# Moving VectorE's operand pieces within the steps of a fused FNet and GEGLU kernel

## The chip, the cores and the metric

The kernel runs on one core of one Trainium2 chip. The metric is the device time of one execution in microseconds (us), from the first to the last instruction with what lies around them. Five engines work side by side, each through its own queue in order: TensorE (PE: matmuls, with PEld for the loads of its weights), VectorE (DVE in the profile, V in the code), ScalarE (ACT, A in the code), GpSimd (POOL, G in the code) and SyncE (SP, which issues the DMAs). They wait for each other through semaphores only.

## The reference

The input x has 2048 rows of 448 floats.

```python
h  = x + real part of DFT_seq(DFT_hidden(layernorm(x)))       # FNet mixing
xn = layernorm(h)
h2 = h + (gelu(xn @ w_gate) * (xn @ w_up)) @ w_down           # 448 -> 1792 -> 448
```

Every operand is split into a high and a low half-precision part, and each product is three matmuls (high·high, high·low, low·high). Most products are Strassen forms, so sums of operand blocks are made and split too.

## The kernel before, in words

The first part (to about 346 us) is the layer norm and the two Fourier transforms; an arranged list of tasks orders it and the change doesn't touch it. Then come 42 gate-and-up steps, written out by hand in the loop `for t in range(N_GU)` (L1552). A step makes one unit of 128 hidden features for a part of the 2048 rows:

- steps 0 to 13 (`q == 0`): the first two quarters of the rows together, matmuls 512 columns wide;
- steps 14 to 27: the third quarter, 256 wide; steps 28 to 41: the fourth.

A step's matmuls go into three PSUM banks X, Y, Z. X and Z are the same two banks in all steps from 14 on. The pieces, with what follows each on another engine:

- `x_open`, `x_close`: X; then ACT takes the gelu of X into `g1` (L1305), and a copy of X into Y (L1291);
- `z_open`: starts Z (L1251 with pZ). It overwrites the bank, so it waits until the step before has read its Z;
- `y_mid`: ACT copies Y into `u3` (L1310), then V adds Z to it (`plus`, L1261; out `hid` or `hh`). This must have read Z before
- `z_close` adds to Z; then V's second `plus` (L1261, out `c`, the tile c12) reads the finished Z; it sets the bank free for the next `z_open`;
- `y_open`, `y_close`: Y; `y_close` is followed by V's L1327 (out `hid` or `hh`);
- `c_last` (ACT, L1335) and `c_mul` (POOL, in steps 15 to 28 V, L1339) finish the second half of the hidden unit in the next step. In steps 0 to 13 the hidden units are stored to DRAM (`store`, L1323, SP's queue) and loaded again in another layout (`hid_load`, L1351).

Between these pieces stand the matmuls of the down product (`dn_mm`, L1191, out `acc_d`). Its rows come in 8 pairs of row tiles, each over 7 chunks of the hidden dimension; chunk d = 7·pair + n needs hidden units n and n + 7. `CHUNK_COUNT` gives each step from 14 on its one or two chunks; in a step PE does 8, 10 and 3 matmuls of each chunk in three places: `some(0, 8)`, `some(8, 18)`, `some(18, 21)`. Pairs 6 and 7 (chunks 42 to 55) are multiplied after step 41. Before PE can take a chunk, three pieces make its operand:

- `dn_sums(d, E)`: two sums 256 wide (L1362, L1363) on POOL, or on V where E is V, and one 128 wide on V (L1364), into `dn_s`, of which there are `DN_S = 3` buffers;
- `dn_hi(d)`: two conversions on ACT (L108, 256 and 640 wide) into `dn_w`;
- `dn_lo(d)`: two subtractions on V (L112, 256 and 640 wide) into `dn_w`; then the `dn_s` buffer is free.

In a step from 14 on, `nexts` are the chunks of the next step (their `dn_lo`, before `some(0, 8)`), `sums` those of the step after it (`dn_sums`, after `y_mid`). Other work hangs on named places of a step: `at(side, (t, k), ...)` puts it there and `do(t, k)` runs it. `ahead_of` (L1494) does so for eight chunks of the pairs 6 and 7: 42 to 47 with t = 30, 32, 34, 36, 38, 40, and 49, 50 with t = 31, 39. Their `dn_sums` is all on V, in step t; `dn_hi` at the end of step t + 1; `dn_lo` in step t + 2 (chunk 47's in step 41, at the end).

For chunks 0 to 3 the pieces stand in steps 11 to 13 of the `q == 0` branch: `hi` and `lo` of the chunks of step t + 2 after `z_close`, and behind them `dn_sums` of those of step t + 3.

Of the kernel before, what the change touches and what calls it, by code (L numbers as in the profile page):

```python
# [17 lines left out]
NF = DF // P  # L18
# [15 lines left out]
def kernel(  # L34
# [38 lines left out]
    V, A, G, PE = nc.vector, nc.scalar, nc.gpsimd, nc.tensor  # L73
# [682 lines left out]
    def at(t, n, *what):  # L756
        t.setdefault(n, []).extend(what)
# [60 lines left out]
    for k, (i, i2) in enumerate(tiles_of):  # L818
        n = where["F", i]
        if k > 1:  # L820
            t = None
            if k > 2:
                t = fixed(n - 10, 8, "SP", 0.5, lambda u=i // 2: x_load(u), lag=4.5, kind="xload")
            first_pair = -40.0 if k == 2 else 0.0
            own = "0" if k == 2 else ""
            if (i, i2) in by_scalar:
                t = [add("A", 1.75, T[max(n - 6, 0)], lambda c=c, both=(i, i2): x_moments(c, both), begin=T[max(n - 7, 0)] - 13.0, after=[t], kind="xstat") for c in (i, i2)]
            else:
                t = [add("V", 1.35, T[max(n - 6, 0)] + first_pair, lambda i=i, j=i2: x_stats(i, j), begin=T[max(n - 7, 0)] - 13.0, after=[t], kind="xstat" + own)]
            lite = (i, i2) in by_scalar  # L830
            t = add("A", 0.5 if lite else 0.3, T[max(n - 5, 0)] + first_pair, lambda i=i, j=i2: x_root(i, j), after=t, kind="xroot" + own)
            t = chain("V", RSTD if lite else (0.2, 0.1, 0.1, 0.1), T[max(n - 5, 0)] + first_pair, lambda i=i, j=i2: x_rstd_steps(i, j), [t], kind="xrstd" + own)
            t = add("V", 0.15, T[max(n - 5, 0)] + first_pair, lambda i=i, j=i2: x_bias(i, j), after=[t], kind="xbias" + own)
# [6 lines left out]
        for c in (i, i2):  # L840
            n = where["F", c]
            done = [steps[n]] if n in steps else [add("N", 0.0, 0.0, lambda: None, begin=(-1.8, 0.0, 0.1)[n])]
            if is_s(c // 2):
                t = drained = add("A", 1.05, T[n + 1] + 1.5, lambda i=c: feature_high(i), after=done + ring_w[-2:][:1] * (len(ring_w) > 1), kind="fhigh")
                t = chain("V", (0.56, 0.36, 0.36), T[n + 2], lambda i=c: feature_sums(i, V), [t], kind="fsum")
                t = add("A", 1.45, T[n + 2] + 2.0, lambda i=c: sums_high(i), after=[t], kind="shigh")
                t = add("V", 1.7, T[n + 2] + 3.5, lambda i=c: sums_low(i), after=[t], kind="slow")
                ring_w.append(t)
            else:
                if n > 1:  # L850
                    t = add("A", 0.95, T[n + 1] + 1.0, lambda i=c: feature_high(i), after=done, kind="fhighp")
                else:
                    t = done[0]
# [42 lines left out]
    for p in range(N_PASS):  # L896
# [18 lines left out]
        if q < 2:  # L915
# [5 lines left out]
            for k in range(2):  # L921
                high = add("A", (0.65, 1.0)[k], t0 + 22.0 + k, lambda q=q, j=j, k=k: ffn_hi(q, j, (k,)), after=[t], kind="hhi")
                t = high
# [435 lines left out]
    def dn_sums(d, E=G):  # L1359
        t = dn_hid(d)  # L1360
        s = dn_s[d] = fpool.tile([P, 5, P], F32, tag="dn_s", bufs=DN_S, name=f"dn_s{d}")
        E.tensor_add(s[:, 0:2], t[:, 0:2], t[:, 2:4])  # L1362
        E.tensor_sub(s[:, 2:4], t[:, 1:4:2], t[:, 0:4:2])  # L1363
        V.tensor_add(s[:, 4], t[:, 0], t[:, 3])  # L1364
# [8 lines left out]
    def dn_hi(d, place=None):  # L1373
        if place is None:
            place = fpool.tile([P, 2, 7, P], F16, tag="dn_w", bufs=4, name=f"dn_w{d}")
        dn_w[d] = place
        for src, dst in dn_parts(d):
            hi_part(place[:, 0, dst], src)

    def dn_lo(d):  # L1380
        w = dn_w[d]
        for src, dst in dn_parts(d):
            lo_part(w[:, 1, dst], src, w[:, 0, dst])
        dn_s.pop(d)
# [54 lines left out]
    def chunks(t):  # L1439
        return CHUNKS.get(t, ())  # L1440
# [4 lines left out]
    def do(t, k):  # L1445
        for what in side.pop((t, k), ()):
            what()
# [44 lines left out]
                at(side, (t0 + f, k), what)  # L1492

    def ahead_of(d, t, place):  # L1494
        at(side, (t, 6), lambda: dn_sums(d, V))
        at(side, (t + 1, 7), lambda: dn_hi(d, place()))
        at(side, (t + 2, 6) if t + 2 < N_GU else (t + 1, 7), lambda: dn_lo(d))

    for n in range(6):
        ahead_of(6 * NC + n, 2 * NF + 2 * n + 2, lambda n=n: spare(n, 6 * NC + n) if n < 4 else None)  # L1500
# [31 lines left out]
    def late_prep(beat):  # L1532
        for f, k in late_beats.pop(beat, ()):
            gu[f].beat(k)
            after = [v for v in LATE if v > f]
            if k == 2 and after:
                gu_late(after[0])
            if k == 1:
                gw[f] = gu[f].w
            if k == 4:  # L1540
                at(late_stores, beat + 1, f)
        for f in late_stores.pop(beat, ()):
            gu[f].store()
# [8 lines left out]
    for t in range(N_GU):  # L1552
        q, f = STEPS[t]
        ahead = {0: (), 11: (14,), 12: (), 13: (15,), 14: (16,)}.get(t, (t + 3,) if t < NF else (t + 2,))
        for s in ahead:
            if s < N_GU and s not in LATE:
                gw_load(s)
        if t in (N_GU - 2, N_GU - 1):
            hr_load(t - N_GU + 8)
        nxt = GateUp(t + 1) if t + 1 < N_GU else None  # L1560
        if q == 0:
            do(t, 0)
            cur.x_close()
            nxt.x_open()
            if prev:
                prev.c_last()
                prev.c_mul()
                prev.store(0)
            cur.y_mid()
            late_prep(2 * t)  # L1570
            do(t, 1)
            down_prep(2 * t)
            if prev:
                prev.store(1)
            nxt.z_open()
            nxt.y_open()
            cur.y_close()
            cur.z_close()
            if t >= 10:
                for d in chunks({10: NF, 11: NF + 1, 13: NF + 2}.get(t)):  # L1580
                    hid_load(d)
            for d in chunks(t + 2):
                done.add(d)
                dn_hi(d)
                dn_lo(d)
            if t < NF - 1:
                for d in chunks(t + 3):
                    dn_sums(d)
            do(t, 2)
            down_prep(2 * t + 1)  # L1590
            late_prep(2 * t + 1)
            do(t, 4)
        else:
            mms = [(d, k) for d in chunks(t) for k in range(21)]

            def some(a, b):
                n = len(chunks(t))
                for d, k in mms[a * n : b * n]:
                    dn_mm(d, range(k, k + 1))

            do(t, 0)
            prev.c_last()
            if t == NF:
                prev.c_mul()
                for g in range(2):
                    prev.store(g)
                half0.close()
                later = ctx.enter_context(tc.tile_pool(name="later", bufs=1, side="right", reuse_waits="tile"))
                hh[2] = [later.tile([P, 4, TQ], F32, name=f"hh2_{n}") for n in range(NC)]
                ops3.append(ring.tile([P, 2, N_OPS, 2 * P], F16, tag="ops", bufs=1, name="ops3"))  # L1610
                hops[3] = ops3[0][:, 0]
            elif t > 2 * NF:
                prev.c_mul()
            for d in chunks(t + 3):
                if d < 4 * NC and t + 3 < 2 * NF + 2 and d not in hid_in:
                    hid_load(d)
            cur.x_close()
            if t > NF:
                cur.z_open()
            nexts = [d for d in chunks(t + 1) if d not in done]  # L1620
            if t == 2 * NF - 1:
                nexts += [d for d in chunks(t + 2) if d < 4 * NC]
            done.update(nexts)
            sums = [d for d in chunks(t + 2) if d not in dn_w and d not in dn_s]
            if t == 2 * NF - 2:
                sums += [d for d in chunks(t + 3) if d < 4 * NC]
            for d in nexts[:1]:
                if d not in dn_w:
                    dn_hi(d)
                dn_lo(d)  # L1630
            for d in nexts[1:]:
                dn_hi(d)
                dn_lo(d)
            some(0, 8)
            if t == 2 * NF:
                quarter2.close()
                last = ctx.enter_context(tc.tile_pool(name="last", bufs=1, reuse_waits="tile"))
                hh[3] = [last.tile([P, 4, TQ], F32, name=f"hh3_{n}") for n in range(NC)]
            cur.y_mid()
            if NF < t <= 2 * NF:  # L1640
                prev.c_mul(V)
            for d in sums:
                dn_sums(d)
            do(t, 6)
            some(8, 18)
            if nxt:
                nxt.x_open()
            do(t, 1)
            if not nxt:
                some(18, 21)  # L1650
            do(t, 4)
            cur.y_close()
            cur.z_close()
            if nxt:
                some(18, 21)
            do(t, 5)
            for d in chunks(t + 2)[:1]:
                if d not in dn_w and t < N_GU - 1:
                    dn_hi(d)
            if nxt:  # L1660
                nxt.y_open()
            do(t, 2)
            do(t, 3)
            do(t, 7)
        prev, cur = cur, nxt
# [108 lines left out]
```

## Time and profile before

| | |
|---|---|
| three runs | 708.01, 708.12, 710.34 us; median 708.12 |
| the profiled execution | 708.02 us, span of its instructions 706.2 us |
| PE | busy 692.6 us of the span (98%), granted clock 1.00 |
| DVE | 586.6 us (83%) |
| ACT | 416.1 us (59%) |
| POOL | 169.6 us (24%) |
| DMA | 196 GB/s in the mean |

PE is busy almost without a break, so what can be won lies in the few places where its queue stands still: for each the profile names the line that PE waited for. A matmul's row ends when its result has drained, which is later than the moment when the next one may start.

### The profile page before, as it was taken

To read this page: it belongs to the slowest core of one execution; us is meant where nothing else is said; L and a number is where in the kernel's file an instruction comes from. 1 tells how busy PE (TensorE), PEld (TensorE's weight loads), DVE (VectorE), ACT (ScalarE), POOL (GpSimd) and SP (SyncE) were. 2 spreads that over 40 slices of the span, in tenths; PEclk is the share of its full clock that TensorE was granted. 3 is DMA by queue.
4 is the path that set the end of the run, shared out by engine and by line. 5 is a ranking of instruction groups with operands and counts; after the bars stand their busy time and mean duration, and the time that the engine had idled before them with its cause. 6 is when DMAs were issued, how large, how long until landed. Compare 5 with 4: busy or idle time off the path is not lost.

```text
span 706.2 us, 14542 instructions
## 1 busy us (share of the span) xinstructions
PE 692.6 (98%) x5644; PEld 544.7 (77%) x5644; DVE 586.6 (83%) x1112; ACT 416.1 (59%) x800; POOL 169.6 (24%) x198
## 2 busy tenths in 40 slices
PE   8999999999999999999999999999999999999998
PEld 5455769888888888888744444479999989889898
DVE  6998999999998999999367987786888866585686
ACT  5789764756765666476357666454554534454442
POOL 0000000000000000000033443444646454545342
PEclk9999999999999999999999999999999999999999
DMA  9444345567696869677558687897785844544301
GB/s 338 143 105 112 84 154 179 197 223 214 200 240 191 241 204 262 229 228 272 206 162 266 224 246 264 263 284 248 199 245 207 259 130 135 181 152 162 131 28 53
DMA packets 95381, 138.77 MB, mean 196 GB/s; under 512 B 42192, under 2 KB 71120, under 8 KB 95312
## 3 DMA queue, kind: packets, MB, share of 16 engines
q1 hardware_dynamic: 95312, 137.85, 62.7%
q8 instruction: 44, 0.72, 0.4%
q14 instruction: 25, 0.20, 0.1%
HBM read 100.99 MB, written 27.53 MB: 182 GB/s over the span
## 4 chain that ended last, share of the span: by engine, by line
PE 80%; DVE 11%; DMA 5%; issue 1%; ACT 1%; SPq 1%; ACTq 0%; DVEq 0%
PE acc L605 29%; PE acc_d L1191 14%; PE pY L1251 13%; PE pZ L1251 9%; PE pX L1251 8%; PE ab L484 7%; DMA wr<-in_w_seq_dram 2%; DVE ws L114 1%; DMA hid_dram<-hid 1%; DVE dn_w L112 1%; DVE wss L114 1%; DVE wsum L549 1%; DVE ops L112 1%; DVE dn_s L1364 1%; DMA x<-in_x_dram 1%
## 5 line engine op out<-in xcount | busy, mean ns | idle before, releaser
L1251 PEld LDWEIGHTS <-gw 128*128 128x128 f16 x1638 | 160.0, 98 | 82.5 <-issue 7.7
L605 PE MATMUL acc<-b,ws 128*128 128x224 f16 (+1 forms) x1248 | 187.1, 288 | 0.0
L605 PEld LDWEIGHTS <-ws 128*128 128x128 f16 x1248 | 120.8, 98 | 35.6 <-DVE ws L114 0.2
L605 PE MATMUL acc<-b,wss 128*128 128x224 f16 x1152 | 141.9, 259 | 1.1 <-DVE wss L114 1.1
L1191 PE MATMUL acc_d<-wd,dn_w 128*128 128x224 f16 x1050 | 115.5, 259 | 0.0
L605 PEld LDWEIGHTS <-wss 128*128 128x128 f16 x1152 | 110.8, 98 | 1.4 <-DVE wss L114 1.4
L1191 PEld LDWEIGHTS <-dn_w 128*128 128x128 f16 x1050 | 101.0, 98 | 1.9
L249 POOL TENSOR_TENSOR wd_s<-wd 128x448 f32<-128x448 f32 x7 | 8.8, 1262 | 376.8 <-DMA wd<-in_w_down_dram 349.1
L1251 PE MATMUL pY<-hops,gw 128*128 128x512 f16 (+1 forms) x476 | 88.8, 326 | 0.0
L108 ACT ACTIVATE wss<-wsum 128x1024 f16<-128x1024 f32 x48 | 50.6, 1055 | 49.6 <-PE acc L605 23.5
L108 ACT ACTIVATE ws<-wr 128x768 f16<-128x768 f32 (+1 forms) x64 | 56.4, 889 | 27.5 <-PE acc L605 13.2
L484 PE MATMUL ab<-wh,xT 128*128 128x448 f16 x352 | 69.1, 352 | 1.4 <-ACT wh L108 0.4
L114 DVE SCALAR_TENSOR_TENSOR ws<-wr,ws 128x768 f16<-128x768 f32 (+1 forms) x64 | 64.9, 1018 | 0.0
L114 DVE SCALAR_TENSOR_TENSOR wss<-wsum,wss 128x1024 f16<-128x1024 f32 x48 | 58.6, 1220 | 6.5 <-ACT wss L108 6.2
L1251 PE MATMUL pZ<-hops,gw 128*128 128x512 f16 (+1 forms) x308 | 59.2, 326 | 1.9 <-DVE hh L1261 1.1
L484 PEld LDWEIGHTS <-xT 128*128 128x128 f16 x352 | 33.9, 98 | 33.5 <-issue 1.9
L1251 PE MATMUL pX<-hops,gw 128*128 128x512 f16 (+1 forms) x308 | 56.9, 326 | 0.0
L112 DVE TENSOR_TENSOR dn_w<-dn_s,dn_w 128x640 f16<-128x640 f32 x50 | 49.9, 998 | 1.8 <-ACT dn_w L108 1.5
L1182 POOL TENSOR_TENSOR hr<-hr,v 128x224 f32<-128x224 f32 x56 | 44.3, 815 | 12.3 <-ACT v L1150 11.9
L1291 ACT ACTIVATE pY<-pX 128x256 f32<-128x256 f32 (+1 forms) x42 | 18.5, 440 | 48.5 <-PE pX L1251 48.5
L108 ACT ACTIVATE dn_w<-dn_s 128x640 f16<-128x640 f32 x50 | 36.5, 729 | 7.7 <-DVE dn_s L1364 6.2
L1261 DVE SCALAR_TENSOR_TENSOR hh<-pZ,u 128x256 f32<-128x256 f32 x28 | 11.8, 420 | 34.4 <-ACT u L1310 34.3
(141 smaller groups left out, 996.1 us busy)
## 6 DMA issues: line engine op xcount, KB each, us to landing
wr<-in_w_seq_dram SPq DMA_DIRECT2D x64, 512.0 KB, 4.4
gw<-w_dram SPq DMA_DIRECT2D x36, 896.0 KB, 5.0
gu_raw<-in_w_gu_dram SPq DMA_DIRECT2D x28, 384.0 KB, 4.2
hid_dram<-hid SPq DMA_DIRECT2D x28, 256.0 KB, 5.0
hid_in<-hid_dram SPq DMA_DIRECT2D x28, 256.0 KB, 5.3
w_dram<-gu_p SPq DMA_DIRECT2D x24, 256.0 KB, 2.7
w_dram<-gw SPq DMA_DIRECT2D x6, 896.0 KB, 5.5
hx<-in_x_dram SPq DMA_DIRECT2D x8, 448.0 KB, 5.2
```

The lines of the kernel that those rows point to most:

```text
L108: A.activation(dst, src, AF.Copy, scale=scale)
L112: V.tensor_sub(dst, src, hi)
L114: V.scalar_tensor_tensor(dst, src, scale, hi, op0=ALU.mult, op1=ALU.subtract)
L249: G.tensor_sub(s[:, 2:4], t[:, 0:2], t[:, 2:4])
L484: PE.matmul(feat[i][r][:, :D], xT[i][:, kx, :], w[:, kw, r * D : (r + 1) * D], start=n == 0, stop=n == 10,)
L549: V.tensor_add(s[:, 0:2], r[:, 0:1].to_broadcast([P, 2, 2 * P]), r[:, 1:3])
L605: PE.matmul(banks[k][:, cols], lhs, rhs, start=k not in begun, stop=stop, skip_group_check=True)
L1182: op(x, x, m)
L1191: PE.matmul(acc[k // 2][:, k % 2 * HD : (k % 2 + 1) * HD], a_of(la, a), b_of(lb, b), start=first and m == 0 and k % 2 == 0, stop=last and ...
L1251: PE.matmul(ps, w[:, wl, wa + ws, :], ops[:, m + ms, :], start=first and n == 0, stop=last and n == len(terms) - 1, skip_group_check=True,)
L1261: V.scalar_tensor_tensor(dst, ps, SC, other, op0=ALU.mult, op1=ALU.add)
L1291: A.activation(self.Y, self.X, AF.Copy)
```

## The change

It moves pieces and changes none of them.

1. `ahead_of`: V's `dn_sums` of the eight chunks goes from the place after `y_mid` (`do(t, 6)`) to the place after `z_close` (`do(t, 5)`, itself moved ahead of `some(18, 21)`, which is PE's alone). Their `dn_lo` goes from `do(t, 6)` to a new place `do(t, 8)` before `some(0, 8)`, so ahead of `y_mid`.
2. Step 27: `hi` and `lo` of chunk 27, formerly third in the list `nexts` ahead of `y_mid`, go behind `z_close` and `do(t, 5)` (the list `behind`). Chunks 25 and 26 stay.
3. Steps 11 to 13: `dn_sums` of chunks 0, 1 goes from the end of step 11 to the place after `y_mid` of step 12, that of chunks 2, 3 from the end of step 12 (behind `lo` of chunks 0, 1) to the place after `y_mid` of step 13.

```diff
     def ahead_of(d, t, place):
-        at(side, (t, 6), lambda: dn_sums(d, V))
+        at(side, (t, 5), lambda: dn_sums(d, V))
         at(side, (t + 1, 7), lambda: dn_hi(d, place()))
-        at(side, (t + 2, 6) if t + 2 < N_GU else (t + 1, 7), lambda: dn_lo(d))
+        at(side, (t + 2, 8) if t + 2 < N_GU else (t + 1, 7), lambda: dn_lo(d))
...
             cur.y_mid()
+            for d in chunks(t + 2):
+                dn_sums(d)
             late_prep(2 * t)
...
                 dn_hi(d)
                 dn_lo(d)
-            if t < NF - 1:
-                for d in chunks(t + 3):
-                    dn_sums(d)
             do(t, 2)
...
             nexts = [d for d in chunks(t + 1) if d not in done]
-            if t == 2 * NF - 1:
-                nexts += [d for d in chunks(t + 2) if d < 4 * NC]
-            done.update(nexts)
+            behind = [d for d in chunks(t + 2) if d < 4 * NC] if t == 2 * NF - 1 else []
+            done.update(nexts + behind)
...
             for d in nexts[1:]:
                 dn_hi(d)
                 dn_lo(d)
+            do(t, 8)
             some(0, 8)
...
             for d in sums:
                 dn_sums(d)
-            do(t, 6)
             some(8, 18)
...
             cur.y_close()
             cur.z_close()
+            do(t, 5)
+            for d in behind:
+                dn_hi(d)
+                dn_lo(d)
             if nxt:
                 some(18, 21)
-            do(t, 5)
```

## The prediction

> **What bounds the kernel now.** I read the page's head first, then the waits of each engine, then the order of time around every wait that TensorE has.
>
> ```profile
> span 706.2 us, 14542 instructions
> PE 692.6 (98%) x5644; PEld 544.7 (77%) x5644; DVE 586.6 (83%) x1112; ACT 416.1 (59%) x800; POOL 169.6 (24%) x198
> ```
>
> PE is the bound. The change touches neither the number nor the shape of an instruction, so it is worth just what it does to PE's standstills. The view of waits, PE's rows:
>
> ```profile
> PE pZ L1251 <- DVE c L1261: 4.4, 4, 1.7
> PE pZ L1251 <- DVE hh L1261: 1.1, 1, 1.1
> PE pZ L1251 <- DVE hid L1261: 0.7, 1, 0.7
> ```
>
> These six are all of PE's waits for VectorE in the 42 steps: four for c12 (the second `plus`, which frees Z for the next `z_open`), two for the first `plus` (which must read Z ahead of `z_close`). The timeline of PE at the places, idle time in brackets:
>
> ```profile
> 575.38 0.71 PE L1251 MATMUL pZ<-hops,gw 128*128 128x256 f16 x5 [1.10 <-DVE hh L1261]
> 614.19 0.81 PE L1251 MATMUL pZ<-ops,gw 128*128 128x256 f16 x6 [0.95 <-DVE c L1261]
> 628.17 0.81 PE L1251 MATMUL pZ<-ops,gw 128*128 128x256 f16 x6 [1.29 <-DVE c L1261]
> 643.42 0.82 PE L1251 MATMUL pZ<-ops,gw 128*128 128x256 f16 x6 [0.54 <-DVE c L1261]
> 657.79 0.82 PE L1251 MATMUL pZ<-ops,gw 128*128 128x256 f16 x6 [1.67 <-DVE c L1261]
> ```
>
> 575.38 is step 27's `z_close`; the other four are the `z_open` of steps 33, 35, 37 and 39, behind the even steps in which `ahead_of` has both a `dn_lo` and a `dn_sums`. Five matmuls make a row of 0.71, six one of 0.82: one adds 0.11, but the last of a row shows about 0.27. So a bracket is 0.16 short of what PE loses, and the five cost 5.55 + 5 × 0.16 = 6.35 us.
>
> **Part 1, the eight chunks of `ahead_of`.** VectorE, ScalarE, POOL and PE in step 32, in that order:
>
> ```profile
> 609.55 0.42 DVE L1261 SCALAR_TENSOR_TENSOR hh<-pZ,u 128x256 f32<-128x256 f32 x1 [2.48 <-ACT u L1310]
> 610.32 0.88 DVE L112 TENSOR_TENSOR ops<-hh,ops 128x256 f16<-128x256 f32 x1
> 611.12 1.28 DVE L112 TENSOR_TENSOR ops<-dn_s,ops 128x640 f16<-128x640 f32 x1
> 612.50 0.43 DVE L1362 TENSOR_TENSOR dn_s<-hh 128x256 f32<-128x256 f32 x1
> 613.39 0.42 DVE L1327 SCALAR_TENSOR_TENSOR hh<-pY,g 128x256 f32<-128x256 f32 x1
> 613.72 0.41 DVE L1261 SCALAR_TENSOR_TENSOR c<-pZ,u 128x256 f32<-128x256 f32 x1
> 614.05 0.42 DVE L112 TENSOR_TENSOR dn_w<-hh,dn_w 128x256 f16<-128x256 f32 x1
> 614.38 0.82 DVE L112 TENSOR_TENSOR dn_w<-dn_s,dn_w 128x640 f16<-128x640 f32 x1
> ...
> 607.04 0.73 ACT L108 ACTIVATE ops<-dn_s 128x640 f16<-128x640 f32 x1
> ...
> 608.15 0.73 POOL L1339 TENSOR_TENSOR hh<-hh,c 128x256 f32<-128x256 f32 x1 [3.87 <-ACT c L1335]
> ...
> 611.04 0.71 PE L1251 MATMUL pZ<-ops,gw 128*128 128x256 f16 x5
> ...
> 618.42 0.71 PE L1251 MATMUL pZ<-ops,gw 128*128 128x256 f16 x5
> ```
>
> PE finishes Z at 611.75, yet c12 starts at 613.72: ahead of it stand chunk 42's `dn_lo` (610.32 to 612.40) and chunk 43's `dn_sums` (612.50 to 613.39). Just before, at the first `plus`, VectorE had stood idle for 2.48 us. The change puts the `dn_lo` into that hole and the `dn_sums` behind c12. The `dn_lo` needs ACT's high part, which is there at 607.77; it takes 1.15 alone (614.05 to 615.20, chunk 33's) or 2.08 beside POOL (610.32 to 612.40), both less than 2.48. Then c12 ends near 612.2, 0.9 before PE wants Z (614.19 − 1.11 = 613.08): the wait goes, here and by the same order in steps 34, 36 and 38. Sum 0.95 + 1.29 + 0.54 + 1.67 + 4 × 0.16 = 5.09 us.
>
> What is late next: the sums now delay what follows c12 on VectorE, the next step's `dn_lo` pieces and then its first `plus`, behind which PE's `z_close` waits. The tightest is step 33, where another `dn_lo` (chunk 49) stands there too. From c12's end at 612.2 to step 33's `z_close` (618.42, moved to 617.3) are 5.1 us; the `plus` takes 0.42 and a little on either side, so 4.6 are left for sums (0.89), chunk 33's `dn_lo` (1.15) and chunk 49's (1.15, or 2.08 beside POOL). That is 3.2 to 4.1: it fits, with 0.5 us in hand at the worst of these rows. The same load comes only in steps 32 and 40 and, with the `dn_lo` of chunks 35 and 36, in step 35. The other directions are covered: the moved chunks are multiplied after step 41, so neither their `dn_hi` a step later nor PE waits; a `dn_s` buffer is now held from c12 of one step to the start of the second next, less long than before. No DMA is issued in these pieces.
>
> How POOL slows VectorE is the weak point. In the rows a subtraction of 0.42 takes 0.88 and one of 0.82 takes 1.28 beside POOL, 0.46 more each. The Trainium skill (SBUF — State Buffer, section "Who interferes with whom") says that a DVE instruction with two SBUF inputs contends with a GpSimd instruction that reads SBUF, and that the second to issue "fully blocks" until the first ends. By that rule a piece could lose a whole POOL instruction of 0.73 each time, and chunk 49's `dn_lo` would take 1.15 + 2 × 0.73 = 2.6, an estimate by that page; step 33 would then need 4.65 of its 4.6, still no loss to speak of. The trace's 0.46 is a part of it, as if the wait began halfway.
>
> **Part 2, chunk 27 in step 27.** VectorE, and ScalarE's `u3`:
>
> ```profile
> 571.51 1.35 DVE L112 TENSOR_TENSOR dn_w<-dn_s,dn_w 128x640 f16<-128x640 f32 x1
> 572.78 0.94 DVE L112 TENSOR_TENSOR dn_w<-hid_in,dn_w 128x256 f16<-128x256 f32 x1
> 573.64 1.34 DVE L112 TENSOR_TENSOR dn_w<-dn_s,dn_w 128x640 f16<-128x640 f32 x1
> 574.91 0.41 DVE L1261 SCALAR_TENSOR_TENSOR hh<-pZ,u 128x256 f32<-128x256 f32 x1
> ...
> 581.22 0.42 DVE L1261 SCALAR_TENSOR_TENSOR hh<-pZ,u 128x256 f32<-128x256 f32 x1 [4.67 <-ACT u L1310]
> ...
> 572.63 0.36 ACT L1310 ACTIVATE u<-pY 128x256 f32<-128x256 f32 x1
> ```
>
> `u3` is ready at 572.99, but the first `plus` stands behind chunk 27's two subtractions until 574.91. Without them it runs at 573.0 and ends at 573.4, before `z_close`'s unhindered start (575.38 − 1.26 = 574.12). The whole 1.10 + 0.16 = 1.26 us goes. Chunk 27's conversions and subtractions land behind c12, two steps before PE takes the chunk; next behind them is the `plus` of step 28, for which VectorE had idled 4.67 us. On ACT the two conversions leave the place ahead of `u3`, which only helps.
>
> **Part 3, chunks 0 to 3.** Here I book nothing, though a wait of 0.72 + 0.16 = 0.88 us goes. In the order of time, the lines are from the timelines of DVE, PE, POOL and ACT, then the chain and the table of stretches:
>
> ```profile
> 462.57 2.09 DVE L1364 TENSOR_TENSOR dn_s<-hid_in 128x128 f32<-128x128 f32 x2
> 482.08 0.29 DVE L1364 TENSOR_TENSOR dn_s<-hid_in 128x128 f32<-128x128 f32 x1 [3.04 <-DMA hid_in<-hid_dram]
> ...
> 465.31 1.24 PE L1251 MATMUL pZ<-hops,gw 128*128 128x512 f16 x5 [0.72 <-DVE hid L1261]
> ...
> 461.92 1.31 POOL L1363 TENSOR_TENSOR dn_s<-hid_in 128x256 f32<-128x256 f32 x1
> 463.19 1.32 POOL L1339 TENSOR_TENSOR hid<-hid,c 128x512 f32<-128x512 f32 x1
> 468.09 1.46 POOL L1339 TENSOR_TENSOR hid<-hid,c 128x512 f32<-128x512 f32 x1 [3.58 <-ACT c L1335]
> ...
> 470.77 7.80 DMA hid_dram<-hid
> 478.65 3.40 DMA hid_in<-hid_dram
> ...
> 483.09 0.82 PE pZ L1251 x6
> ...
> 460.00:465.00 5.00, 4.59 (x31) 2.84 (x29) 5.00 (x7) 3.55 (x8) 3.40 (x3) 1.00 1.01 344
> ```
>
> In step 13 the sums of 2.09 us delay the first `plus`; moved behind it they free `z_close` (465.31). But 18 us later PE stands at 483.09 (step 16's `z_open`) at the end of another chain: unit 13's store at 470.77, 7.80 us of DMA, the load of chunk 6 (3.40), its sum on VectorE at 482.08, c12, `z_open`. That chain hangs on SP's queue and on the DMA engines, busy share 1.01 from 460 to 465 us, not on PE. PE arrives there 0.88 us earlier and waits 0.88 longer. The pieces before it are on VectorE and POOL in steps 12 and 13, so the same chain hides what they may cost, as long as unit 13's product on POOL (to 469.55 now) is done by 470.77. It may slip: the sums of chunks 2 and 3 (now all behind POOL's product of unit 12, which moves up from 463.19 towards 461.9) and so ACT's conversions stand ahead of its gelu. By POOL's rows two chunks take at most 4 × 1.31 = 5.2 us from 463.2, to 468.4, and with a conversion and the gelu (about 0.7 each) the product would end at 471.3: at most 0.5 us late. Bounds: a loss of 0.5, or, if the DMAs move up with unit 12's store, a gain of 0.88; I take zero, since the DMA share shows a full queue.
>
> **The sum.** 5.09 + 1.26 + 0 = 6.35 us. The profiled execution took 708.02, of it 706.2 span: 708.02 − 6.35 = 701.67. It lies 0.1 under the median of the three runs; I forecast 701.7.
>
> **The rivals.**
>
> *The join gains too.* If unit 12's product, 1.3 us earlier on POOL, pulls the store, the load and the next store with it, part 3 keeps its 0.88: 700.8. Against it stands the full DMA queue.
>
> *VectorE is only partly freed.* The moved pieces make the first `plus` late in the tight steps 32, 33, 35 and 40, by as much as the 0.5 in hand is overrun. Were all three pieces beside POOL (sums 0.89 + 3 × 0.46 = 2.27, `dn_lo` 2.08 twice), 6.4 us would stand against 4.6: 1.8 lost in each, and if two of the four do so, 3.6: 705.3. For it: POOL runs three instructions per such step; against it: they start only after ACT's gelu, when most of VectorE's pieces are past.
>
> *The other side, slower.* VectorE loses a whole 0.73 us to POOL in each of the seven pieces (three sums, four subtractions) between c12 and the next first `plus`: 3.2 + 5.1 = 8.3 us against 4.6, 3.7 lost in each of the four steps, 14.8 in all: 708.0 − 6.35 + 14.8 = 716.5. It turns into a loss where the overrun passes 6.35 / 4 = 1.6 us a step, four whole waits and more. This is the blocking rule of the skill page above taken to its end. Against it, no row between 606 and 616 us lost over 0.46, and POOL hasn't seven instructions there.
>
> **How the numbers follow.** The forecast as it stands, 701.0 to 702.8 by the half us at the join and some tenths in tight steps: 0.72. The join gains too: 0.12. Partly freed: 0.12. Slower: 0.04. Leaving out the slow case and the upper half of the partly freed one, the range is 700.5 to 703.6. A measurement of this kernel can tell 0.5%, 3.5 us, from no change: faster than 704.6 are the first two cases and half of the third, 0.90; within 0.5% 0.06; slower 0.04.
>
> **What would show it.** In the trace after: PE's waits for `c` and for `hh` gone from 566 us on; VectorE's `dn_lo` ahead of the first `plus` in the even steps, its 256-wide sums behind c12. In step 13 `z_close` without a wait, and a wait near 483 us of about 0.9, ended by VectorE, with chunk 6's load landing near 482. The prediction is wrong if new PE waits for `hh` stand in steps 32, 33, 35 or 40, or if the load of chunk 6 lands more than half a us off.

## The result and the profile after

| | before | after |
|---|---|---|
| median of 5 runs, us (lowest to highest) | 708.46 (708.01 to 711.46) | 703.44 (701.63 to 705.16) |
| ratio of the times, 95% interval | | 0.9907 [0.9882, 0.9932] |
| profiled execution, us | 708.02 | 701.63 |
| its span, us | 706.2 | 699.9 |

The time fell by 0.93%. The median lies inside the range of 700.5 to 703.6, near its upper end, and above the 701.0 to 702.8 of the forecast as it stands. The profiled execution fell by 6.39 us against the 6.35 of the sum. The median lies 1.8 us above that execution: both kernels' five runs scatter by about 3.5 us, more than the three that the prediction started from.

The head of the page after, TensorE's waits of the 42 steps in the view of waits (total, times, longest), and the timeline of PE at step 15's and step 16's `z_open`, at step 27's `z_close` and at the `z_open` and `z_close` of step 33:

```profile
span 699.9 us, 14545 instructions
PE 691.3 (99%) x5644; PEld 544.8 (78%) x5644; DVE 581.6 (83%) x1112; ACT 416.0 (59%) x800; POOL 169.6 (24%) x198
...
PE pZ L1251 <- DVE c L1261: 1.2, 1, 1.2
...
474.79 0.81 PE L1251 MATMUL pZ<-hops,gw 128*128 128x256 f16 x6 [1.22 <-DVE c L1261]
...
483.06 0.82 PE L1251 MATMUL pZ<-hops,gw 128*128 128x256 f16 x6
...
574.10 0.71 PE L1251 MATMUL pZ<-hops,gw 128*128 128x256 f16 x5
...
611.79 0.82 PE L1251 MATMUL pZ<-ops,gw 128*128 128x256 f16 x6
616.03 0.71 PE L1251 MATMUL pZ<-ops,gw 128*128 128x256 f16 x5
```

Of the six waits of before none is left, and one that was not there has come: 474.79, which is step 15's `z_open`, with chunk 5's sum late. Lining up PE's 5644 matmuls before and after, one by one, gives what each place won: 0.88 at step 13's `z_close`, −1.38 at step 15's `z_open` (bracket 1.22 and 0.16), 0.25 at step 16's `z_open`, 1.26 at step 27's `z_close`, and 1.11, 1.45, 0.70 and 1.83 at the `z_open` of steps 33, 35, 37 and 39. With 0.27 that PE was already ahead before 455 us, where nothing is changed, that is 6.37 us. (Below, "shift" always means this: the start of the same matmul in two traces.)

Why the new wait is where it is, VectorE's timeline of after around it and, below it, that of before with PE's row:

```profile
469.69 0.29 DVE L1364 TENSOR_TENSOR dn_s<-hid_in 128x128 f32<-128x128 f32 x1
473.18 0.29 DVE L1364 TENSOR_TENSOR dn_s<-hid_in 128x128 f32<-128x128 f32 x1 [3.20 <-DMA hid_in<-hid_dram]
...
474.33 0.41 DVE L1261 SCALAR_TENSOR_TENSOR c<-pZ,u 128x256 f32<-128x256 f32 x1
```

```profile
472.47 0.29 DVE L1364 TENSOR_TENSOR dn_s<-hid_in 128x128 f32<-128x128 f32 x1 [0.64 <-DMA hid_in<-hid_dram]
...
473.62 0.41 DVE L1261 SCALAR_TENSOR_TENSOR c<-pZ,u 128x256 f32<-128x256 f32 x1
...
474.56 0.82 PE L1251 MATMUL pZ<-hops,gw 128*128 128x256 f16 x6
```

Before, c12 started at 473.62 and could have released PE 0.46 later (that is the distance 474.33 to 474.79 after), at 474.08; PE came at 474.56: 0.48 us in hand. After, PE comes 1.15 earlier (the 0.88 and the early 0.27) and c12 0.71 later, with its sum: 1.15 + 0.71 − 0.48 = 1.38. The 0.71 comes from a load, as SP's timelines show, before and then after (hid_dram is unit 12's stores, hid_in the loads of chunks 4 and 5; the second of each pair is issued at the end of its row):

```profile
460.94 4.12 SPq L1323 DMA_DIRECT2D hid_dram<-hid  x2
465.15 4.01 SPq L1351 DMA_DIRECT2D hid_in<-hid_dram  x2
```

```profile
460.78 2.74 SPq L1323 DMA_DIRECT2D hid_dram<-hid  x2
463.61 5.80 SPq L1351 DMA_DIRECT2D hid_in<-hid_dram  x2
```

```profile
461.70 1.28 POOL hid L1339
...
463.00 6.04 DMA hid_dram<-hid
...
469.09 4.00 DMA hid_in<-hid_dram
```

The last fence is the chain of waits after: unit 12's product on POOL, its store, chunk 5's load, and behind it the sum at 473.18. The store is issued 1.5 us earlier than before (the first row of SP ends at 463.5, not at 465.1), and still chunk 5's load is issued no sooner (the second row ends at 469.4, not at 469.2). The store landed at 469.03, before the change at 468.79: the DMA engines took the 1.5 us whole.

### The profile page after: what moved, and what is told of

Its sections match the earlier page's. It is cut to its first block, busy times and chain, and to the rows that moved or that the text cites. A ratio compares the mean times of both kernels' runs of the same rounds, so it can differ in the third digit from the quotient of the medians.

```text
span 699.9 us, 14545 instructions
## 1 busy us (share of the span) xinstructions
PE 691.3 (99%) x5644; PEld 544.8 (78%) x5644; DVE 581.6 (83%) x1112; ACT 416.0 (59%) x800; POOL 169.6 (24%) x198
## 4 chain that ended last, share of the span: by engine, by line
PE 84%; DVE 6%; DMA 6%; issue 1%; SPq 1%; ACT 1%; POOL 1%; ACTq 0%; DVEq 0%
PE acc L605 30%; PE acc_d L1191 16%; PE pY L1251 14%; PE pZ L1251 9%; PE pX L1251 9%; PE ab L484 7%; DMA wr<-in_w_seq_dram 2%; DVE ws L114 1%; DMA hid_dram<-hid 1%; DVE wss L114 1%; DMA hops<-xs 1%; DVE wsum L549 1%; DMA x<-in_x_dram 1%; DMA xT<-xs 1%; DMA hid_in<-hid_dram 1%
## 5 line engine op out<-in xcount | busy, mean ns | idle before, releaser
L1182 POOL TENSOR_TENSOR hr<-hr,v 128x224 f32<-128x224 f32 x56 | 42.7, 787 | 12.3 <-ACT v L1150 11.9
L1310 ACT ACTIVATE u<-pY 128x256 f32<-128x256 f32 (+1 forms) x42 | 19.1, 454 | 34.8 <-PE pY L1251 34.7
```

The costliest lines, as they stand in the source:

```text
L1182: op(x, x, m)
L1310: A.activation(u3, self.Y, AF.Copy, scale=SC)
```

## The experiments

Four parts of one theory were to be told apart: that each removed wait is paid out at its own place (parts 1 and 2 of the prediction), that part 3's is given back at a chain of DMAs, that VectorE has room for the moved pieces in the tight steps, and what ends that chain.

**The three parts, each alone.** `e1_ahead` has only `ahead_of`'s edits, `e2_step27` only the list `behind`, `e3_join` only the `dn_sums` of chunks 0 to 3; the rest is as before.

```diff
# e1_ahead, against the kernel before
-        at(side, (t, 6), lambda: dn_sums(d, V))
+        at(side, (t, 5), lambda: dn_sums(d, V))
-        at(side, (t + 2, 6) if t + 2 < N_GU else (t + 1, 7), lambda: dn_lo(d))
+        at(side, (t + 2, 8) if t + 2 < N_GU else (t + 1, 7), lambda: dn_lo(d))
# e2_step27
+            for d in behind:       # behind z_close, formerly in nexts
+                dn_hi(d)
+                dn_lo(d)
# e3_join
             cur.y_mid()
+            for d in chunks(t + 2):
+                dn_sums(d)
```

> The kernel before with part 1 alone (the eight chunks' sums behind c12, their dn_lo ahead of the first plus). Theory that PE's waits simply add up: the four waits at the z_open of steps 33, 35, 37 and 39 go and nothing else does; PE's start after step 39 lies 5.09 us earlier than before (1.11 + 1.45 + 0.70 + 1.83), the span near 701.1, a time near 703.0 where the kernel before has 708.1. Rival that parts 1 and 2 overlap (step 27's wait, left in, leaves more slack later): less than 4.5 us.

> The kernel before with part 2 alone (chunk 27's hi and lo behind step 27's z_close). Adding up: step 27's wait of 1.10 goes, 1.26 us with the matmul's drain, the four later waits stay as they were (0.95, 1.29, 0.54, 1.67); span near 704.9, time near 706.8. Rival: the time won at step 27 comes back in a longer wait of steps 33 to 39, then about 708.

> The kernel before with part 3 alone (the sums of chunks 0 to 3 moved). If the DMA chain sets the time: step 13's z_close no longer waits (PE 0.88 us earlier at 465 us), and by 484 us PE is where it was, within 0.3: no change, about 708.1. If the part costs by itself on VectorE and POOL: step 16's z_open more than 0.5 us later than before, 708.7 or more. If the join gains: 707.3.

| | median, us (runs) | ratio to before | places won, by shift, us |
|---|---|---|---|
| `e1_ahead` | 705.23 (11) | 0.9929 [0.9907, 0.9951] | 1.12, 1.45, 0.70, 1.83 |
| `e2_step27` | 707.84 (12) | 0.9974 [0.9954, 0.9994] | 1.26 |
| `e3_join` | 709.22 (12) | 1.0001 [0.9978, 1.0024] | 0.88, then −1.23 and 0.25 |

The savings add up within the intervals: 0.71% and 0.26% and nothing, against 0.93% for the whole. Parts 1 and 2 are worth what the brackets said, each at its own places; part 3 by itself is no change that can be measured, for the 0.88 is given back nine microseconds later. (The trace of `e2_step27` has two further waits, of 0.52 and 0.36 by shift, at the `z_open` of steps 15 and 16, where it changes nothing, and in that of `e1_ahead` step 27's wait, which it doesn't touch, is 0.51 longer.) The wait that takes it, in the timeline of PE of `e3_join`, and then the same place in `e1_ahead`, where part 3 is not done, with VectorE's sum of chunk 5 ahead of it:

```profile
474.19 0.82 PE L1251 MATMUL pZ<-hops,gw 128*128 128x256 f16 x6 [1.07 <-DVE c L1261]
```

```profile
476.30 0.29 DVE L1364 TENSOR_TENSOR dn_s<-hid_in 128x128 f32<-128x128 f32 x1 [3.02 <-DMA hid_in<-hid_dram]
...
477.91 1.44 PE L1251 MATMUL pZ<-hops,gw 128*128 128x256 f16 x6 [3.49 <-DVE c L1261]
```

So in the profiled execution of `e1_ahead` the same place stood for 3.49 us with the old sums: chunk 5's load was late there by itself (its sum stands at 476.30, where it stood at 472.47 before). The place belongs to the load, and part 3 is one way among others to reach it. That execution of `e1_ahead` took 708.18, 3 us over the median of its own kernel.

**Two ways to take the chain away.** If the wait at step 15 is the DMA queue's, it should go when the queue is lighter. `e4_hr_late` issues the first residual pair's load (448 KB, line 1407, between the stores in step 13) in step 16. If it is only that c12 stands behind the sums, it should go when the sums stand behind c12: `e5_sums_behind` does that with the `dn_sums` of steps 14 and 15. `e6_both` does both.

```diff
# e4_hr_late, against the kernel after
-        at(side, (t0 - 4, 0), lambda p=p: hr_load(p))
+        at(side, (t0 - 4, 0) if p else (t0 - 1, 4), lambda p=p: hr_load(p))
# e5_sums_behind
             for d in sums:
-                dn_sums(d)
+                if t > NF + 1:
+                    dn_sums(d)
...
             cur.z_close()
+            for d in sums:
+                if t <= NF + 1:
+                    dn_sums(d)
             do(t, 5)
```

> The changed kernel with the load of the first residual pair (hr, 448 KB) issued at step 16 instead of step 13. If the full DMA queue ahead of unit 12's store sets the wait at step 15's z_open: its packets (1.4 to 1.5 us of the queue) no longer stand ahead of the store, the load of chunk 5 lands about 1.4 us earlier, the wait of 1.22 (1.38 with the drain) goes to 0 to 0.3, and the span falls from 699.9 to about 698.5, a time near 700.2. If the store's own latency or SP's queue sets it, or the 896 KB weight load ahead of it does: no change (699.9).

> The changed kernel with the sums of chunks 4, 5 and 6 (steps 14 and 15) moved behind c12 as well, so that VectorE no longer stands at a load ahead of c12. If the wait at step 15's z_open comes only from the place of chunk 5's sum in VectorE's queue: that wait (1.38) and step 16's go although the load lands as before; PE 1.4 to 1.6 us earlier after step 16 than the changed kernel, unless ScalarE, which converts chunk 6 ahead of u2, takes 0.3 to 0.6 back: span 698.3 to 699.0. Rival (the late load holds PE by its matmuls): the wait turns up at acc_d of step 16 and the span stays near 699.9.

> The changed kernel with both: hr's first load at step 16 and the sums of chunks 4 to 6 behind c12. Both take away the same wait, so no more than either alone: PE after step 16 1.4 to 1.7 us earlier than in the changed kernel, no wait of PE from 455 us on, median 701.0 to 702.3 where the kernel before has 709.8 in these rounds. If late loads are what spreads the times, the spread of the runs gets smaller than that of the changed kernel (3.5 us over five).

Medians 702.51 (6 runs), 701.97 (4) and 701.81 (5), ratios to before 0.9890 [0.9864, 0.9916], 0.9904 [0.9884, 0.9923] and 0.9895 [0.9876, 0.9913]. In none of the three traces does PE wait at all from 455 us to the end. Step 15's `z_open` and, for the first, chunk 4's and 5's sums on VectorE, now in one row without a wait between them; for the second, VectorE with c12 ahead of the sums:

```profile
471.75 1.21 DVE L1364 TENSOR_TENSOR dn_s<-hid_in 128x128 f32<-128x128 f32 x2
475.50 0.82 PE L1251 MATMUL pZ<-hops,gw 128*128 128x256 f16 x6
```

```profile
473.09 0.42 DVE L1261 SCALAR_TENSOR_TENSOR c<-pZ,u 128x256 f32<-128x256 f32 x1 [0.19 <-PE pZ L1251]
473.44 0.53 DVE L1364 TENSOR_TENSOR dn_s<-hid_in 128x128 f32<-128x128 f32 x2
474.60 0.82 PE L1251 MATMUL pZ<-hops,gw 128*128 128x256 f16 x6
```

In all three the wait is gone. That c12 stands behind the sum is shown by `e5_sums_behind`: the load lands there at 473.58, no sooner than in the kernel after (473.08), and c12 no longer waits for it. The queue's half is less sure. In `e4_hr_late` PE came to this place 2.09 us later than in the kernel after, from waits far ahead of the edit, and that alone eases the wait (in `e9_lo_twice`, 1.65 later with nothing changed here, 0.59 of the 1.22 is left); the store landed at 469.13, no sooner than the 469.03 of after, and only the load behind it was shorter (2.8 us from issue to landing, not 4.0). In `e6_both` PE was on time, the store took 4.0 us in place of 6.0, and the load landed at 469.77, which speaks for the queue. But in a second execution of that kernel (`e12_both_again`, below) the store took 6.2 us again and the load landed at 472.13, only 0.95 us sooner than in the kernel after. So the residual load may be part of what holds chunk 5's load up; how much of it, these traces don't settle. The ratios can't tell the three from the kernel after (0.9907); what the wait's end is worth is read from the traces: `e6_both` has a span of 698.3, 1.6 below. In the profiled executions of `e4_hr_late` and `e5_sums_behind` (spans 700.6 and 699.7) some more waiting ahead of 280 us, where nothing is changed, takes it again: about 1 us of it (1.5 in the first) near 276.

**More load on the queue.** `e10_hr_two` is the dose in the other direction: the second residual pair's load too is issued in step 13.

```diff
-        at(side, (t0 - 4, 0), lambda p=p: hr_load(p))
+        at(side, (t0 - 4, 0) if p != 1 else (NF - 1, 0), lambda p=p: hr_load(p))
```

> The changed kernel with the second residual pair's load (448 KB) also issued in step 13. If the queue ahead of unit 12's store sets the wait at step 15's z_open, 1.4 to 1.5 us of packets more stand in it: the wait of 1.38 grows to 2.8 to 2.9, the span to about 701.3, unless other waits differ. If not the queue: 1.2 to 1.6 as before.

707.01 us (one run), span 705.2. Views of `e10_hr_two`: SP, PE, and stretches of 1 us, where PEclk is the last column but two:

```profile
461.52 2.04 SPq L1407 DMA_DIRECT2D hr<-h_dram  x2
...
465.15 8.66 SPq L1351 DMA_DIRECT2D hid_in<-hid_dram  x2
...
478.75 1.44 PE L1251 MATMUL pZ<-hops,gw 128*128 128x256 f16 x6 [3.64 <-DVE c L1261]
...
478.00:479.00 1.00, 0.24 (x2) 0.18 (x2) 0.70 (x3) 0.93 (x2) 0.71 (x2) 0.64 0.93 373
479.00:480.00 1.00, 1.00 (x7) 0.69 (x6) 0.48 (x2) 1.00 (x3) 0.00 (x0) 0.50 1.04 319
480.00:481.00 1.00, 1.00 (x7) 0.83 (x6) 0.83 (x2) 1.00 (x4) 0.00 (x0) 0.50 0.69 205
```

The place and the direction are as the queue's theory has them: the row of the loads is 8.66 long in place of 5.80, and the wait is 3.64 in place of 1.22. The size is not: 2.4 us more, where 1.4 to 1.5 were expected. And `e1_ahead` waited 3.49 here without the second load, so this one trace doesn't show that the load did it: the scatter of chunk 5's load alone reaches as far. And the standstill was followed by a half clock, of which below.

**The two moves of `ahead_of`.** Which of them frees c12? `e7_lo_only` moves just the `dn_lo`, `e8_sums_only` just the sums (the two halves of `e1_ahead`'s diff).

> The kernel before with only the dn_lo of the eight chunks ahead of the first plus, their sums left where they were. By VectorE's rows the sums alone (0.9 to 2.0 us from the first plus on) are over before PE has finished Z: all four waits go, 5.0 to 5.1 us, as with both moves. Rival (each piece is half of the delay): 2 to 3 us left of the waits.

> The kernel before with only the sums of the eight chunks behind c12, their dn_lo left after the first plus. By the rows the dn_lo (2.1 us beside POOL) ends at 612.4 in step 32 and 626.4 in step 34 (two sums ahead of it): c12 then ends about 0.1 late for step 33 and 0.5 late for step 35, the others in time: 4.4 to 4.5 us of the 5.09. Rival: 2 to 3 us.

705.31 and 703.38 us (one run each). By the shifts at steps 33, 35, 37 and 39, `e7_lo_only` wins 0.94, 0.93, 0.70 and 1.20, together 3.77: the expectation missed. `e8_sums_only` wins 1.07, 1.06, 0.70 and 1.79 and loses 0.17 at step 35's `z_close`: 4.45, as expected. The two overlap (3.77 + 4.45 is far over 5.09), so either does most of the work, and only both do all. What the first lacks, VectorE and PE in step 34 of `e7_lo_only`:

```profile
623.34 0.42 DVE L1261 SCALAR_TENSOR_TENSOR hh<-pZ,u 128x256 f32<-128x256 f32 x1 [0.93 <-ACT u L1310]
623.68 1.57 DVE L1364 TENSOR_TENSOR dn_s<-hh 128x128 f32<-128x128 f32 x2
625.17 0.94 DVE L1362 TENSOR_TENSOR dn_s<-hh 128x256 f32<-128x256 f32 x1
...
626.37 0.28 DVE L1364 TENSOR_TENSOR dn_s<-hh 128x128 f32<-128x128 f32 x1
...
627.37 0.81 PE L1251 MATMUL pZ<-ops,gw 128*128 128x256 f16 x6 [0.35 <-DVE c L1261]
```

With the `dn_lo` gone the sums start right behind the first `plus` and run beside POOL: two small ones of other chunks take 1.57 (one alone takes 0.28, the last row but one), and the three of V 1.48, from 625.17 to 626.65, not the 0.89 of step 32, where they stood behind the `dn_lo`.

**How much room the tight steps have.** `e9_lo_twice` does every moved `dn_lo` twice, the second time writing the same values over the first: nothing is left out, and VectorE's load at the disputed place rises.

```diff
-        ... else (t + 1, 7), lambda: dn_lo(d))
+        ... else (t + 1, 7), lambda: (dn_lo_again(d), dn_lo(d)))
```

> The changed kernel with the moved dn_lo of the eight chunks done twice (the same values written again): 1.15 to 2.1 us more on VectorE ahead of the first plus in steps 32, 33, 34, 36, 38, 40 and 41. By the changed kernel's rows the plus may come 1.06 us later in step 32 and 1.6 to 2.7 us later in the others (its idle time before, and 1.06 from its end to z_close). So PE waits for hh in step 32 by 0.1 to 1.1, in step 33 by at most 0.5, nowhere else: span 0.1 to 1.6 us longer. Rival (POOL blocks VectorE for whole instructions, so that the pieces already fill their room): waits in most of the seven steps, over 3 us.

First the place in the kernel after, VectorE in step 33:

```profile
610.92 0.42 DVE L1362 TENSOR_TENSOR dn_s<-hh 128x256 f32<-128x256 f32 x1
...
613.19 0.81 DVE L112 TENSOR_TENSOR dn_w<-dn_s,dn_w 128x640 f16<-128x640 f32 x1
614.55 0.42 DVE L1261 SCALAR_TENSOR_TENSOR hh<-pZ,u 128x256 f32<-128x256 f32 x1 [0.54 <-ACT u L1310]
```

Then `e9_lo_twice`: POOL's product in step 32, VectorE's pieces in step 33, PE's `z_close`, the clock behind it:

```profile
607.90 2.52 POOL L1339 TENSOR_TENSOR hh<-hh,c 128x256 f32<-128x256 f32 x1 [3.53 <-ACT c L1335]
...
611.94 0.79 DVE L1362 TENSOR_TENSOR dn_s<-hh 128x256 f32<-128x256 f32 x1
612.65 0.88 DVE L1363 TENSOR_TENSOR dn_s<-hh 128x256 f32<-128x256 f32 x1
...
616.86 0.95 DVE L112 TENSOR_TENSOR dn_w<-hh,dn_w 128x256 f16<-128x256 f32 x1
617.73 1.27 DVE L112 TENSOR_TENSOR dn_w<-dn_s,dn_w 128x640 f16<-128x640 f32 x1
618.92 0.41 DVE L1261 SCALAR_TENSOR_TENSOR hh<-pZ,u 128x256 f32<-128x256 f32 x1
...
619.39 0.70 PE L1251 MATMUL pZ<-ops,gw 128*128 128x256 f16 x5 [2.17 <-DVE hh L1261]
...
620.40:621.40 1.00, 1.00 (x7) 0.72 (x6) 1.00 (x3) 0.09 (x1) 0.00 (x0) 0.50 0.99 371
```

707.42 us (one run), span 705.6. Of the steps with a double `dn_lo` only step 33 makes PE wait, by 2.33 where at most 0.5 was expected; step 32, expected to, doesn't, and the rival, waits in most of the steps, isn't seen. In the kernel after, the pieces behind c12 last 3.1 us (610.92 to 614.00) and then VectorE waits 0.54 for ACT; the `plus` ends 1.06 before PE's 616.03, so there are 1.6 in hand. With the double `dn_lo` the same stretch lasts 7.0 (611.94 to 618.92), 3.9 more: 2.3 over, and 2.33 is what PE waited. By VectorE's rows the added pair of subtractions is 2.13 of the 3.9; the sums took 0.85 longer than in the kernel after (0.79 and 0.88 in place of 0.42 each) and the pair of the last rows 0.92 longer. I read the lengthening as contention with POOL, which lies beside these pieces: its product of step 32 (0.73 both in the prediction's row and in the kernel after) took 2.52 while VectorE had subtractions back to back, and so POOL's next pieces came to lie beside VectorE's sums.

**Once more, side by side.** `e11_after_again` is the kernel after and `e12_both_again` is `e6_both`, unchanged, on one chip.

> The changed kernel again, on the chip of the next: 0.9907 of the kernel before, as it was, a median 5 to 7 us under it; the wait at step 15's z_open between 0.5 and 3.5 from run to run.

> The kernel with both join repairs again, beside the changed one: 1.4 to 1.7 us less than it in the profile; in the medians 1 to 3 us less, since late loads no longer hold PE.

703.05 (6 runs; 0.9906 [0.9876, 0.9935]) and 701.29 (6; 0.9881 [0.9853, 0.9909]). The second is the best of all the kernels here by 1.8 us on that chip, but the intervals overlap. In the profile it is 0.9 us shorter (699.5 against 700.4), less than the 1.4 to 1.7 expected. Nor does it scatter less: by 4.3 us, and `e6_both` by 2.9, where the kernel after scatters by 3.5 and 3.7. That late loads spread the times, as the expectation of `e6_both` had it, isn't borne out. The traces show what is left in each, first of `e11_after_again`, then of `e12_both_again`:

```profile
474.32 0.82 PE L1251 MATMUL pZ<-hops,gw 128*128 128x256 f16 x6 [0.69 <-DVE c L1261]
483.57 0.82 PE L1251 MATMUL pZ<-hops,gw 128*128 128x256 f16 x6 [0.81 <-DVE c L1261]
```

```profile
482.12 0.42 ACT L108 ACTIVATE dn_w<-hid_in 128x256 f16<-128x256 f32 x1 [2.72 <-DMA hid_in<-hid_dram]
483.83 0.74 ACT L108 ACTIVATE dn_w<-dn_s 128x640 f16<-128x640 f32 x1 [1.29 <-POOL dn_s L1363]
...
484.88 0.82 PE L1251 MATMUL pY<-hops,gw 128*128 128x256 f16 x6 [0.84 <-ACT u L1296]
```

The kernel after again waits for loads, this time at two places, at 483.57 also for chunk 6, the one that the prediction had named. With both edits a late chunk 6 no longer holds up c12, but ACT, which converts it ahead of step 16's `u`: a load that is late enough holds up the next instruction that stands behind it (1.00 us by shift).

## Why the prediction was right, and where it was not

*Part 1, 5.09 us.* Won 1.11, 1.45, 0.70 and 1.83, with the reason given. The assumption that a bracket falls 0.16 short of what PE loses holds at each of these places. Three of its sizes were off. The 0.5 us in hand at step 33 was 1.6, since neither of the two `dn_lo` there ran beside POOL. The tightest step was 35, which the prediction names beside it: its `plus` ends at 627.94, 0.63 before PE's `z_close`. "Sums 0.89" was read where they stood behind other pieces; beside POOL they took 1.48 (`e7_lo_only`). And the 0.46 that POOL was taken to cost was typical (the last subtraction before step 32's `plus` took 1.36, not 0.82) but not the most. The same form, on VectorE and then POOL in step 14 of the kernel after:

```profile
467.51 1.89 DVE L112 TENSOR_TENSOR dn_w<-dn_s,dn_w 128x640 f16<-128x640 f32 x1
...
467.18 1.55 POOL L1339 TENSOR_TENSOR hid<-hid,c 128x512 f32<-128x512 f32 x1 [1.37 <-ACT c L1335]
```

It lost 1.07 beside a POOL product of 1.55 that started 0.33 ahead of it, and ended 0.67 after it. The ends tell more than the starts. In the prediction's fence the subtraction of 0.82 ends at 612.40, 0.69 after POOL's piece beside it (line 1182, 610.20 to 611.71); in step 32 of the kernel after one ends at 608.28, 0.68 after POOL's product (606.87 to 607.60). So each of them ended as if it had stood until POOL's piece was over and then taken most of its own time: the 0.46 was what was left of POOL's piece, not a wait that began halfway. This agrees with the whole block that the Trainium skill (SBUF — State Buffer, "Summary: rules for kernel authors") states for a DVE instruction with two SBUF inputs beside a GpSimd one that reads SBUF, and not with the "part of it" that the prediction read. By the rule of the same page of the Trainium skill ("Who interferes with whom") that the order of issue decides who blocks, POOL loses in its turn, as `e9_lo_twice` had it. None of this cost PE anything in the kernel after.

*Part 2, 1.26 us.* Won 1.26, in the kernel after and alone.

*Part 3, nothing.* The mechanism held: PE arrived earlier and waited for a load that did not move up. The place didn't: "18 us later PE stands at 483.09" looked only at the next wait that was already there. Nine microseconds later stood a place with 0.48 in hand, less than the 0.88 that PE was to win, and of the same kind (a store, a load, a sum, c12). So the whole 0.88 and 0.50 more was lost at 474.79, the old wait of 0.25 at 483 went, and the term is −0.25, inside its bounds of −0.5 to 0.88. The sign that was named, a wait of about 0.9 near 483 us, didn't come, though chunk 6's load landed where it did before (481.86, and 482.06 before). "Unit 13's product may slip, at most 0.5 late" did not happen (POOL's row above ends at 468.73, and at 469.55 before); the half microsecond came from the DMA engines instead. The rival "the join gains too" fails with the 1.5 us of the earlier store that came to nothing.

*The sum.* That the profiled execution meets it within 0.04 us is luck: part 3's −0.25, booked as nothing, was made good by the 0.27 that PE was early before the change begins. What the moved pieces won themselves is 6.10.

*The other rivals.* Neither "VectorE is only partly freed" nor the slower one is seen: PE has no wait for `hh` in steps 32, 33, 35 and 40. `e9_lo_twice` shows that the mechanism exists and what it takes: 3.9 us more on VectorE, not the lengthening that POOL gives by itself.

*The median.* 1.7 above the forecast. The sum was made against one execution at the low end of its runs, 708.02, and gave 701.67 for one at the low end of the runs after, 701.63. What the other runs have more is not traced. The traces of `e1_ahead` and `e11_after_again` show late loads of chunks 5 and 6, and others an extra 1 us near 276, as sources of such a scatter; how much of it they make stays open.

## What to carry to other kernels

In these traces a wait behind an in-order queue was won in full when the piece ahead of it fitted into a hole of the same engine that is seen in the trace. Count the wait by the start of what follows, and time the moved piece beside whatever POOL runs there. Before booking it, follow the gain forward: not only to the next wait, but to every place whose operand comes from a DMA and which has less in hand than the gain. If such a place is there, move the consumer of the load behind what the bound engine needs, as `e5_sums_behind` does; a lighter DMA queue may help too, but here it did so unevenly.

## What the hardware showed that I had not expected

A long standstill of PE costs more than itself. Behind 3.49 us in `e1_ahead` and 3.64 us in `e10_hr_two` PE's granted clock was 0.50 for about 3.4 us, most of which the stretches above show (0.64, 0.50 and 0.50), matmuls in rows of six took 1.44 in place of 0.82, and the shift grew by another 1.6 and 1.4 us. The Trainium skill (TensorE: Matmul & The Clock Gate, "Part 1: The HAM clock gate") gives half rate after an idle window of about 3.4 us, and the length of the half clock agrees with that figure. But in `e9_lo_twice` 2.33 us of standstill were enough, with the half clock starting 1 us after PE was back, and the shift there grew from 3.36 to 5.02 us while it lasted. The 1.67 us before and the 1.38 after had no such sequel.

The length of one standstill doesn't decide it, though. `e9_lo_twice` has another half clock, from 9.41 to 12.83 us. The clock had risen at 6.00, and no bracket between is over 0.97; `e12_both_again` has 0.96 at the same matmul and keeps its clock. PE's longest standstill there and a stretch of the half clock:

```profile
7.74 0.23 PE L445 MATMUL xT_ps<-ident,xs 128*128 128x128 f16 x1 [0.97 <-DVE xs L112]
...
10.00:11.00 1.00, 1.00 (x4) 0.44 (x3) 0.59 (x2) 1.00 (x2) 0.00 (x0) 0.50 1.07 414
```

The clock records of the traces show a grid instead: between two changes of the clock lie whole multiples of 3.413 us (138, 1 and 66 of them in `e1_ahead`; 1, 1, 178, 1 and 24 in `e9_lo_twice`), and the grid begins at another moment in each execution. The standstill of step 33 in `e9_lo_twice` lies whole within one piece of it, 616.99 to 620.40, and the clock fell at that piece's end, 1 us after PE was back. How much of a piece PE must stand idle isn't settled: the 1.67 before also lay whole within one.

And a store that was issued 1.5 us earlier into a queue whose engines were busy (share 1.01 before) landed no earlier: its time from issue to landing rose from 4.2 to 6.0 us.
